# Range tests made in the second layer's stage on data loaded a second time, no clamps, and border decays multiplied on VectorE

## The chip, the cores and the metric

The kernel runs on one NeuronCore of a Trainium2 chip. The core has five engines that run side by side and wait for each other through semaphores: TensorE (PE in the profile; its weight loads are PEld), VectorE (DVE), ScalarE (ACT), GpSimd (POOL) and SyncE (SP), which here only starts DMA transfers. The metric is the device time of one launch in microseconds (us), as a median of three runs.

## The reference

Three blocks follow each other. The first is a linear attention with a complex decay: 4 batches, 8 heads, 768 steps, head size 48. The two others are feed-forward layers on the 3072 x 384 result.

```
mag = sqrt(a_re^2 + a_im^2);  scale = min(mag, 0.999) / (mag + 1e-6)
S   = (a * scale)_t * S + k_t v_t^T          # complex state per head, 48 x 48
y_t = q_t . Re(S)
g   = elu(y @ w_in);    x2  = g @ w_out                         # d_ff 2048
h   = max(x2 @ w1, x2 @ w2, x2 @ w3);  out = h @ w_out2         # d_ff 768
```

## The kernel before

**Attention.** Time is cut into chunks of 128 steps; a pair of chunks of one batch is a group `n` (12 groups), and its chunks are `(n, 0)` and `(n, 1)`. In each group the decay is turned into a logarithm and an angle (`sq`, `m2`, `lns`, `inv0` to `inv2`, `rho`, `wexp`, `lnr`, `arctan`), both are summed along time with a matmul (`cum_t`, `cum_l`), and `q` and `k` are multiplied by exp(+-) of the sums and by cosine and sine (`emul`, `hat`). Then come the transposes, masked scores, the state and the output `y`, which `x_split` writes as two fp32r halves into the tile `x` of the first layer. Between neighbouring chunks the state is scaled by a border decay: `rate` writes half of it, `gain` multiplies it twice with a row of exp tiles (tile `gt`, 32 x 384), sends one row to DRAM (`gd`) and reads it back as the tile `g` (48 x 8, two transfers), which `state_out` needs.

**First layer.** Columns of 256 tokens (block `b`, 12 of them, one per group) go through 16 weight tiles `w0` to `w15`. A step `(b, j)` uses two of them: `h_pair` (line 705) makes the hidden values, `elu` and `elu_split` turn them into `g`, `o_pair` (line 748) adds into `x2`. Weights arrive as 64-bit words; `dec1` puts each together on VectorE (`word`, lines 190 to 197), copies it on ScalarE (line 83) and subtracts the copy (line 204).

**Range tests.** The fast path holds only while the decays lie in a range and the weights have exponents in a range. `chk_re` and `chk_im` are ScalarE operations with an accumulated sum into `flags`; the test of a weight is a VectorE operation on its top bytes (line 212, tile `dm`) and a ScalarE sum into `small`. `clamp` (line 266) and `clamp_im` (line 273) on VectorE hold `re` and `im` inside the range for the work that follows. At the end all marks are added, and a general version of the program runs if one is set.

**Second layer.** `m_step(b, f)` (line 957) makes three banks of 128 x 512 with 27 matmuls, `ScalarE` copies the first (tile `t`), VectorE takes the maximum with the second and the third (lines 965, 966), and the result is split into the tile `m`. Even and odd `f` use different sets of three PSUM banks. `out_step(b)` (line 981) is 72 matmuls in four groups, each copied out by ScalarE (tile `o`) from one of two banks. There are 6 blocks of 512 tokens and 6 tiles `f`; six larger weight tiles (`wb`, 1536 KB each) are decoded at the end of the first layer and at the start of the second.

**Order.** The first group is written out by hand. The others follow the table `STEPS`: each row names a relative step and functions of it, and `work_until` calls them between the steps of the first layer. What comes out is put in order by a scheduler, engine by engine, and each engine then works through its own list in that order. All transfers are started by SP, in order too: a transfer whose target buffer is still in use holds back the ones listed after it.

Of the kernel before, what the change touches and what calls it, by code (L numbers as in the profile page):

```python
# [9 lines left out]
F32 = mybir.dt.float32  # L10
F32R = mybir.dt.float32r
U32 = mybir.dt.uint32
U8 = mybir.dt.uint8
I32 = mybir.dt.int32
AF = mybir.ActivationFunctionType
ALU = mybir.AluOpType
# [4 lines left out]
P = 128  # L21
W = H * D
# [3 lines left out]
NF1, NF2, NK = FF1 // P, FF2 // P, DM // P  # L26
NT = B * S
RE_LO, IM_HI = 0.8, 0.75
# [5 lines left out]
NWA, NWB = 2 * DM, 3 * NK * P + DM  # L34
# [58 lines left out]
def tile_kernel(  # L93
# [14 lines left out]
    nc = tc.nc  # L108
    act = ActQueue(tc)
# [3 lines left out]
    wp = pa.enter_context(tc.tile_pool(name="wp", bufs=1))  # L113
    mp = pa.enter_context(tc.tile_pool(name="mp", bufs=2))
# [3 lines left out]
    T = {}  # L118
# [3 lines left out]
    def at(shape, tag, dt=F32, bufs=1, name=None):  # L122
        return ap.tile(shape, dt, tag=tag, name=name or tag, bufs=bufs)
# [39 lines left out]
    def const_col(x, name):  # L163
        t = cp.tile([P, 1], F32, name=name)
        nc.vector.memset(t, x)
        return t

    b_w = const_col(math.log(2e-6), "b_w")
    b_re = const_col(RE_LO, "b_re")
    b_im = const_col(-IM_HI * IM_HI, "b_im")  # L170
    b_pi2 = const_col(math.pi / 2, "b_pi2")
    flags = cp.tile([P, 2 * NG], F32, name="flags")
# [13 lines left out]
    def word(raw, t):  # L186

        hw, lw = raw[:, :, 1], raw[:, :, 0]
        u = t.bitcast(U32)
        nc.vector.tensor_scalar(  # L190
            out=u, in0=hw, scalar1=0x07FFFFFF, scalar2=3,
            op0=ALU.bitwise_and, op1=ALU.logical_shift_left,
        )
        nc.vector.scalar_tensor_tensor(
            out=u, in0=hw, scalar=0xC0000000, in1=u, op0=ALU.bitwise_and, op1=ALU.bitwise_or
        )
        nc.vector.scalar_tensor_tensor(  # L197
            out=u, in0=lw, scalar=29, in1=u, op0=ALU.logical_shift_right, op1=ALU.bitwise_or
        )

    def split_w(wpool, t, n, tag):
        wt = wpool.tile([P, 2, n], F32R, tag=tag, name="w")
        act.copy(wt[:, 0, :], t)
        nc.vector.tensor_tensor(  # L204
            out=wt[:, 1, :], in0=t, in1=wt[:, 0, :].bitcast(F32), op=ALU.subtract
        )
        return wt

    def decode(wpool, raw, n, tag, t, m, col):

        top = raw.rearrange("p n t -> p (n t)").bitcast(U8).rearrange("p (n t) -> p n t", t=8)
        nc.vector.tensor_scalar(
            out=m, in0=top[:, :, 7], scalar1=0x78, scalar2=0x38,
            op0=ALU.bitwise_and, op1=ALU.bitwise_xor,
        )
        act.activation(m, m, AF.Identity, accum_out=small[:, col:col + 1])
        word(raw, t)
        return split_w(wpool, t, n, tag)

# [34 lines left out]
    def new(nm, n):  # L254
        if (nm, n) not in T:
            T[nm, n] = at([P, 2, W], nm)
        return T[nm, n]

    def of(nm, n, c):
        t = new(nm, n)  # L260
        return t if c is None else t[:, c, :]

    def clamp(n, c=None, to=None):
        if ("rec", n) not in T:
            T["rec", n] = T["re", n] if to is None else to
        nc.vector.tensor_scalar(
            out=of("rec", n, c), in0=of("re", n, c), scalar1=RE_LO, scalar2=2.0**30,
            op0=ALU.max, op1=ALU.min,
        )

    def clamp_im(n, c=None):
        x = of("im", n, c)
        nc.vector.tensor_scalar(
            out=x, in0=x, scalar1=-IM_HI, scalar2=IM_HI, op0=ALU.max, op1=ALU.min
        )

    def sq(n, c=None):
        act.activation(of("m2", n, c), of("rec", n, c), AF.Square)
        act.activation(of("aux", n, c), of("im", n, c), AF.Square)

    def m2(n, c=None):
        x = of("m2", n, c)
        nc.vector.tensor_tensor(out=x, in0=of("aux", n, c), in1=x, op=ALU.add)

    def chk_im(n, to=None):
        act.activation(
            new("aux", n) if to is None else to, T["aux", n], AF.Relu, bias=b_im,
            accum_out=flags[:, 2 * n + 1:2 * n + 2],
        )

    def chk_re(n, to=None):
        act.activation(
            new("aux", n) if to is None else to, T["re", n], AF.Relu, bias=b_re, scale=-1.0,
            accum_out=flags[:, 2 * n:2 * n + 1],
        )

    def lns(n, c=None):
        act.activation(of("aux", n, c), of("rec", n, c), AF.Ln)
# [111 lines left out]
    def gain(n, c):  # L410
        if ends(n, c):
            return
        n2, c2 = after(n, c)
        sl = bslice(c)
        t = T["gt", n2]
        nc.gpsimd.tensor_tensor(out=t[sl], in0=t[sl], in1=T["em", n2, c2][sl], op=ALU.mult)  # L416
        nc.gpsimd.tensor_tensor(out=t[sl], in0=t[sl], in1=T["ep", n, c][sl], op=ALU.mult)
        row = P - 1 if c == 0 else 0
        ci = 2 * n + c
        nc.sync.dma_start(gd[ci], t[row:row + 1, :])  # L420
        g = at([96, H], "g", bufs=2)
        for j in (0, 1):
            T["dma"] = nc.sync.dma_start(
                g[j * D:(j + 1) * D, :], gd[ci].rearrange("o (h d) -> d (o h)", h=H)
            )
        T["g", ci] = g
# [225 lines left out]
    def state_out_in(n):  # L652
# [2 lines left out]
    STEPS = {  # L655
        -31: ([(load_re,)], []),
        -29: ([(load_im,)], []),
        -28: ([(chk_re,)], [(clamp,)]),
        -27: ([(sq,)], [(m2,)]),
        -26: ([(chk_im,)], [(clamp_im,)]),  # L660
        -25: ([], [(win_ln,)]),
        -24: ([(inv0,), (inv1,)], [(inv2,)]),
        -22: ([(wexp,), (rho,)], []),
# [29 lines left out]
    w1 = {}  # L693
    raw = {}
# [73 lines left out]
    def dec1(f):  # L768
        if f % 2:
            t = at([P, NWB], "tb")[:, :NWA]  # L770
        else:
            t = mp.tile([P, NWA], F32, tag="dt", name="dt", bufs=1)
        m = mp.tile([P, NWA], U8, tag="dm", name="dm", bufs=1)
        w1[f] = decode(wp, raw[f], NWA, f"w{f}", t, m, f)

    raw2, pools, wbt = {}, {}, []

# [3 lines left out]

    def split_wb(f):
        t, m = (bp.tile([P, NWB], d, tag=x, name=x) for x, d in (("dt", F32), ("dm", U8)))
        wbt.append(decode(pools[f], raw2[f], NWB, f"wb{f}", t, m, NF1 + f))

    def load_x2(b, pool):
        t = bp.tile([P, 4, NK * P], F32, tag="xr", name="xr", bufs=1)
        nc.sync.dma_start(t, x2d[4 * b:4 * b + 4].rearrange("c p n -> p c n"))
        x = pool.tile([P, 2, NK, 4, P], F32R, tag="xx", name="xx", bufs=1 if pool is bp else 2)
        tv = t.rearrange("p c (m t) -> p m c t", m=NK)  # L790
        T["xx", b] = x
        for m in range(NK):
            act.copy(x[:, 0, m], tv[:, m])
            nc.vector.tensor_tensor(
                out=x[:, 1, m], in0=tv[:, m], in1=x[:, 0, m].bitcast(F32), op=ALU.subtract
            )
# [50 lines left out]
            score(0, c, hf)  # L847
            mask(0, c, hf)

    keep_re = at([P, 2, W], "nr")  # L850
    junk = at([P, 2, W], "lnr")
    for c in (0, 1):
        clamp(0, c, keep_re)
        sq(0, c)
        m2(0, c)
    chk_im(0, junk)
    with act.window():
        both(lns)
    for f in (inv0, inv1, inv2, clamp_im, rho):
        both(f)  # L860
    both(wexp)
    chk_re(0, junk)
    load_re(1)
    load_im(1)
    load_more(0, RAW1)
# [73 lines left out]
    bq = pm.enter_context(tc.tile_pool(name="bq", bufs=1))  # L939
# [34 lines left out]
    def out_step(b):  # L974
        for i in range(4):
            bank = ps.tile([P, 512], F32, tag="a", name="ob", bufs=2)
            ts = slice(i * P, (i + 1) * P)
            for f in range(NF2):
                mt = T["m", b, f]
                for s, (wt, mi) in enumerate(((0, 0), (1, 0), (0, 1))):  # L980
                    nc.tensor.matmul(  # L981
                        bank[:, :DM], lhsT=mt[:, mi, ts], rhs=wbt[f][:, wt, NWB - DM:],
                        start=f == 0 and s == 0, stop=f == NF2 - 1 and s == 2,
                    )
            o = bq.tile([P, DM], F32, tag="o", name="o", bufs=3)
            act.copy(o, bank[:, :DM])
            nc.sync.dma_start(out[(4 * b + i) * P:(4 * b + i + 1) * P, :], o)

    NB2 = NT // 512
    half = range(NF2 // 2)  # L990
    for b in (0, 1):
        for f in half:
            m_step(b, f)
            if b == 0:
                split_wb(3 + f)
    for b in range(NB2):
        for f in range(NF2 // 2 if b < 2 else 0, NF2):
            m_step(b, f)
            if b and f == (NF2 // 2 if b == 1 else 1):
                out_step(b - 1)  # L1000
            if f == NF2 // 2 and 2 <= b + 1 < NB2:
                load_x2(b + 1, bq)
    out_step(NB2 - 1)

    count = NG * 2
# [3 lines left out]
        out=sums, in0=sums, scalar=0.0, in1=ones[:, :count], op0=ALU.mult, op1=ALU.add  # L1009
# [3 lines left out]
        out=flags, in0=flags, scalar=0.0, in1=sums, op0=ALU.not_equal, op1=ALU.add  # L1013
# [300 lines left out]
```

## Time and profile before

| | |
|---|---|
| median of 3 runs | 948.45 us (947.55 to 948.99) |
| the profiled execution | 947.95 us, of which 946.2 us are the span from the first to the last instruction |
| TensorE busy | 897.1 us (95%), weight loads 818.5 us (87%) |
| VectorE, ScalarE, GpSimd busy | 611.7 us (65%), 527.6 us (56%), 58.2 us (6%) |
| mean granted TensorE clock | 0.986 of full speed |
| DMA | 77.39 MB, mean 82 GB/s |

A busy share is a mean over stages with different limits, so the stages are read one by one: up to about 141 us the first groups of attention and the decoding of the weights go on while TensorE gets its first work; up to 640 us attention and the first layer run together; from 640 us on it is the second layer alone. Matmuls are pipelined, and a busy TensorE is not TensorE at its peak. The granted clock has two levels, 1.2 and 2.4 GHz; 1.00 in a row is 2.4 GHz throughout.

### The profile page before, as it was taken

How to read it: one execution, taken by the hardware profiler on the slowest of the kernel's cores; microseconds unless marked ns; L12 is line 12 of the kernel's file. 1: busy time of each engine (PE TensorE's matmuls, PEld its weight loads, DVE VectorE, ACT ScalarE, POOL GpSimd, SP SyncE). 2: the span in 40 equal slices, each digit the busy share in tenths (PEclk: the TensorE clock that was granted, in tenths of full speed). 3: DMA queues.
4: the chain of work that ended last, by engine and by line, in shares of the span. 5: the costliest groups of instructions: out<-in, count | busy, mean ns of one | idle time of the engine just before them, and what ended most of it. 6: DMA issues, size and time to landing. Idle time of an engine off the chain costs nothing.

```text
span 946.2 us, 19146 instructions
## 1 busy us (share of the span) xinstructions
PE 897.1 (95%) x8036; PEld 818.5 (87%) x8036; DVE 611.7 (65%) x938; ACT 527.6 (56%) x857; POOL 58.2 (6%) x45
## 2 busy tenths in 40 slices
PE   4568989999999999999999999999999999999997
PEld 1448879999999999999999999998888989898886
DVE  6997999988877897878786753687822141322221
ACT  8988888876766786766763633665312121221111
POOL 0110120011100120200020200000000000000000
PEclk9987989999999999999999999999999999999999
DMA  8642011253333333333323212616101102000001
GB/s 320 263 182 79 1 46 46 72 139 90 100 81 96 80 96 79 97 80 96 79 63 80 63 46 52 250 35 250 34 9 42 50 1 66 2 26 9 17 17 38
DMA packets 63943, 77.39 MB, mean 82 GB/s; under 512 B 22100, under 2 KB 51944, under 8 KB 63080
## 3 DMA queue, kind: packets, MB, share of 16 engines
q1 hardware_dynamic: 63848, 76.08, 26.4%
q8 instruction: 65, 1.06, 0.5%
q14 instruction: 30, 0.25, 0.1%
HBM read 52.43 MB, written 9.47 MB: 65 GB/s over the span
## 4 chain that ended last, share of the span: by engine, by line
PE 84%; DVE 7%; ACT 6%; DMA 1%; issue 1%; POOL 1%; SPq 0%; DVEq 0%; ACTq 0%; POOLq 0%
PE mb L957 24%; PE x L748 20%; PE h L705 19%; PE ob L981 8%; PE a L585 4%; PE a L530 4%; PE a L553 3%; PE a L352 1%; ACT L78 1%; ACT aux L78 1%; DVE w L204 1%; DVE lnr L328 1%; PE a L527 1%; DVE dt L197 1%; ACT dm L78 1%
## 5 line engine op out<-in xcount | busy, mean ns | idle before, releaser
L705 PE MATMUL h<-x,w 128*128 128x256 f32 x1728 | 233.5, 287 | 5.7 <-ACT w L83 3.0
L748 PE MATMUL x<-g,w 128*128 128x256 f32 x1728 | 233.9, 287 | 0.1
L705 PEld LDWEIGHTS h<-x,w 128*128 128x128 f32 x1728 | 218.5, 193 | 11.7 <-ACT w L83 3.6
L748 PEld LDWEIGHTS x<-g,w 128*128 128x128 f32 x1728 | 217.4, 192 | 9.0 <-issue 6.5
L957 PE MATMUL mb<-xx,w 128*128 128x512 f32 x972 | 224.8, 392 | 0.0
L957 PEld LDWEIGHTS mb<-xx,w 128*128 128x128 f32 x972 | 182.4, 188 | 40.8
L78 ACT ACTIVATE e<-h 128x512 f32<-128x512 f32 x96 | 56.9, 593 | 85.8 <-PE h L705 85.1
L965 DVE TENSOR_TENSOR t<-mb,t 128x512 f32<-128x512 f32 x36 | 24.9, 690 | 122.0 <-PE mb L957 122.0
L716 DVE SCALAR_TENSOR_TENSOR e<-e,h 128x512 f32<-128x512 f32 x96 | 65.1, 678 | 43.7 <-ACT e L78 43.5
L83 ACT CAST m<-t 128x512 fp32r<-128x512 f32 x36 | 22.4, 621 | 119.7 <-DVE t L966 119.7
L83 ACT CAST g<-e 128x512 fp32r<-128x512 f32 x96 | 59.2, 616 | 47.3 <-DVE e L716 47.1
L725 DVE TENSOR_TENSOR g<-e,g 128x512 fp32r<-128x512 f32 x96 | 65.8, 685 | 19.5 <-ACT g L83 19.2
L981 PE MATMUL ob<-w,m 128*128 128x384 f32 x432 | 76.4, 337 | 0.0
L981 PEld LDWEIGHTS ob<-w,m 128*128 128x128 f32 x432 | 75.6, 188 | 0.5
L78 ACT ACT_TABLE_LOAD x54 | 69.3, 1283 | 1.7 <-PEq L1298 0.7
L78 ACT ACTIVATE e<-e 128x512 f32<-128x512 f32 x96 | 60.7, 632 | 2.2
L416 POOL TENSOR_TENSOR gt<-gt,em 32x384 f32<-32x384 f32 x20 | 31.0, 1548 | 473.1 <-ACT em L78 428.1
L966 DVE TENSOR_TENSOR t<-mb,t 128x512 f32<-128x512 f32 x36 | 24.9, 691 | 39.4 <-PE mb L957 39.4
L83 ACT COPY o<-ob 128x384 f32<-128x384 f32 x24 | 11.5, 479 | 59.3 <-PE ob L981 59.3
L530 PE MATMUL a<-qkt 96*32 96x128 f32 x1152 | 38.9, 276 | 0.7 <-DVE p L539 0.7
L83 ACT COPY t<-mb 128x512 f32<-128x512 f32 x36 | 21.1, 586 | 33.1 <-PE mb L957 24.6
L969 DVE TENSOR_TENSOR m<-t,m 128x512 fp32r<-128x512 f32 x36 | 24.9, 691 | 20.3 <-ACT m L83 20.3
(114 smaller groups left out, 1052.1 us busy)
## 6 DMA issues: line engine op xcount, KB each, us to landing
qkt<-tb SPq DMA_DIRECT2D x216, 64.0 KB
raw<-in_wa_dram SPq DMA_DIRECT2D x16, 768.0 KB
raw<-in_wb_dram SPq DMA_DIRECT2D x6, 1536.0 KB
v<-in_v_dram SPq DMA_DIRECT2D x24, 256.0 KB
q<-in_q_dram SPq DMA_DIRECT2D x12, 384.0 KB
k<-in_k_dram SPq DMA_DIRECT2D x12, 384.0 KB
x2d<-x SPq DMA_DIRECT2D x36, 128.0 KB
xr<-x2d SPq DMA_DIRECT2D x6, 768.0 KB
```

Source lines behind the costliest of these rows:

```text
L78: ins = self.nc.scalar.activation(out, in_, func, **k)
L83: self.nc.scalar.copy(out, in_)
L416: nc.gpsimd.tensor_tensor(out=t[sl], in0=t[sl], in1=T["em", n2, c2][sl], op=ALU.mult)
L530: nc.tensor.matmul(o[32 * s:32 * s + 32], lhsT=k1[:, s], rhs=q1, start=True, stop=True, tile_position=(0, 32 * s),)
L553: nc.tensor.matmul(bank[:96, h * D:(h + 1) * D], lhsT=kh[:, h, :], rhs=vt[:, o:o + D], start=True, stop=True,)
L585: nc.tensor.matmul(bank[32 * quad:32 * quad + 32, o * P:(o + 1) * P], lhsT=lhs, rhs=rhs, start=start, stop=stop, tile_position=(0, 32 * quad),
L705: nc.tensor.matmul(bank[:, i * BT:(i + 1) * BT], lhsT=w[:, wi, wsl], rhs=xb[b][:, xi, kk, :], start=m == 0, stop=m == 8,)
L716: nc.vector.scalar_tensor_tensor(out=e, in0=e, scalar=-1.0, in1=bank, op0=ALU.add, op1=ALU.max)
L725: nc.vector.tensor_tensor(out=g[:, 1], in0=e, in1=g[:, 0].bitcast(F32), op=ALU.subtract)
L748: nc.tensor.matmul(x2[m], lhsT=w[:, wi, wsl], rhs=g[:, gi, i * BT:(i + 1) * BT], start=j + i + s == 0 and b > 1, stop=j == NP - 1 and i == ...
L957: nc.tensor.matmul(bank, lhsT=wbt[f][:, wt, o:o + P], rhs=x[:, xi, kk].rearrange("p c t -> p (c t)"), start=m == 0, stop=m == 8,)
L981: nc.tensor.matmul(bank[:, :DM], lhsT=mt[:, mi, ts], rhs=wbt[f][:, wt, NWB - DM:], start=f == 0 and s == 0, stop=f == NF2 - 1 and s == 2,)
```

## The change

Three things are changed. The functions `clamp`, `clamp_im`, `chk_re` and `chk_im` go; the tile `rec` is now `re` itself. The test of the first layer's weights leaves `decode` (now `fit`). In the second layer's stage, all of `a_re` and `a_im` (12 groups of twice 384 KB) and the first layer's 16 weight tiles (768 KB each) are loaded once more, and the tests are made there: per group two ScalarE operations with a sum and one square, per weight tile one VectorE and one ScalarE operation. And `gain` multiplies on VectorE. The tests of the second layer's own weights stay where they were.

```
-    def decode(wpool, raw, n, tag, t, m, col):
+    def fit(raw, m, col):
         top = raw.rearrange("p n t -> p (n t)").bitcast(U8).rearrange("p (n t) -> p n t", t=8)
         nc.vector.tensor_scalar(
             out=m, in0=top[:, :, 7], scalar1=0x78, scalar2=0x38,
             op0=ALU.bitwise_and, op1=ALU.bitwise_xor,
         )
         act.activation(m, m, AF.Identity, accum_out=small[:, col:col + 1])
+    def decode(wpool, raw, n, tag, t):
         word(raw, t)
         return split_w(wpool, t, n, tag)
...
     def sq(n, c=None):
+        T["rec", n] = T["re", n]
...
-        nc.gpsimd.tensor_tensor(out=t[sl], in0=t[sl], in1=T["em", n2, c2][sl], op=ALU.mult)
-        nc.gpsimd.tensor_tensor(out=t[sl], in0=t[sl], in1=T["ep", n, c][sl], op=ALU.mult)
+        nc.vector.tensor_tensor(out=t[sl], in0=t[sl], in1=T["em", n2, c2][sl], op=ALU.mult)
+        nc.vector.tensor_tensor(out=t[sl], in0=t[sl], in1=T["ep", n, c][sl], op=ALU.mult)
...
-        -28: ([(chk_re,)], [(clamp,)]),
         -27: ([(sq,)], [(m2,)]),
-        -26: ([(chk_im,)], [(clamp_im,)]),
...
-        w1[f] = decode(wp, raw[f], NWA, f"w{f}", t, m, f)
+        w1[f] = decode(wp, raw[f], NWA, f"w{f}", t)
...
+    again, fits = [], list(range(NF1))
+    def load_again():
+        f = len(again)
+        if f < NF1:
+            t = bq.tile([P, NWA, 2], U32, tag="again", name="again", bufs=3)
+            nc.sync.dma_start(t.rearrange("p n t -> p (n t)"), wa[:, f, :].bitcast(U32))
+            again.append(t)
+    def in_range(n):
+        for i, src in enumerate((a_re, a_im)):
+            t = bq.tile([P, 2, W], F32, tag=f"rng{i}", name="rng", bufs=2)
+            nc.sync.dma_start(t, src[n])
+            mark = flags[:, 2 * n + i:2 * n + i + 1]
+            if i == 0:
+                act.activation(t, t, AF.Relu, bias=b_re, scale=-1.0, accum_out=mark)
+            else:
+                act.activation(t, t, AF.Square)
+                act.activation(t, t, AF.Relu, bias=b_im, accum_out=mark)
+    def fit_again():
+        if fits:
+            f = fits.pop(0)
+            fit(again[f], bq.tile([P, NWA], U8, tag="fm", name="fm", bufs=2), f)
+            load_again()
...
+            if b == 1 and f >= NF2 // 2:
+                load_again()
+            if b > 1:
+                fit_again()
+                if f % 2:
+                    in_range((b - 2) * NF2 // 2 + f // 2)
```

Three places show what the scheduler makes of it. The first is ScalarE in the first stage, group 0, from the second table load on (`lnr,flags` and `aux,flags` are `chk_re`, `dm,small` is the test of a weight, `th` the arctan, `gt` the border rate):

```order
 L78 ACT_TABLE_LOAD
 L78 ACTIVATE aux<-aux 128x384 x2
-L78 ACTIVATE lnr,flags<-re,b_re 128x768
-L78 ACTIVATE dm,small<-dm 128x768
-L78 ACTIVATE aux<-m_125,b_w 128x384 x2
+L78 ACTIVATE aux<-m_122,b_w 128x384 x2
 L78 ACT_TABLE_LOAD
 L78 ACTIVATE th<-th 128x384 x2
 L78 ACT_TABLE_LOAD
 L78 ACTIVATE gt<-lnr 32x384 x2
-L78 ACTIVATE aux,flags<-re,b_re 128x768
```

The tests are gone from between the steps of the decay; the two operations on `m` follow the exponentials directly.

The second place is SP's list of transfers at the first border decay (`gd` and `g` are its way through DRAM, `k` and `q` the inputs of group 1, `raw` the first layer's weights):

```order
 L181 DMA raw<-in_wa_dram 128x1536 x6
-L420 DMA gd<-gt 1x384
-L423 DMA g<-gd 48x8x1 x2
+L398 DMA gd<-gt 1x384
+L251 DMA k<-in_k_dram 128x768
+L247 DMA q<-in_q_dram 128x768
+L401 DMA g<-gd 48x8x1 x2
 L181 DMA raw<-in_wa_dram 128x1536 x8
```

The loads of `k` and `q` for group 1 now stand between the write of `gd` and the reads of `g`, and ahead of eight weight tiles that they stood behind.

The third place is ScalarE of the changed kernel in the second layer, at the ends of the fourth and fifth `m_step` (`t<-mb` frees a PSUM bank, `m<-t` splits a result, `rng` are the tests on the data loaded again):

```order
L83 COPY t<-mb 128x512
L83 CAST m<-t 128x512
L78 ACTIVATE rng,flags<-rng,b_re 128x768
L78 ACTIVATE rng<-rng 128x768
L78 ACTIVATE rng,flags<-rng,b_im 128x768
L78 ACTIVATE rng,flags<-rng,b_re 128x768
L83 COPY t<-mb 128x512
L78 ACTIVATE rng<-rng 128x768
L83 CAST m<-t 128x512
L78 ACTIVATE rng,flags<-rng,b_im 128x768
L83 CAST w<-dt 128x1536
L78 ACTIVATE rng,flags<-rng,b_re 128x768
```

The first tests stand as early as the fifth `m_step`, between the copies that free banks; the last of them stands behind the first copy `o` of the second `out_step`, and all 16 weight tests lie in the same stretch.

## Rows read from the trace of the kernel before

**Rows 1.** Windows: PE, PEld, DVE, ACT, POOL busy (instructions), PEclk, DMA share, GB/s

```profile
0.00:50.50 50.50, 26.61 (x192) 16.79 (x192) 41.26 (x70) 45.12 (x73) 3.90 (x7) 1.00 0.79 300
50.50:94.60 44.10, 32.78 (x320) 28.89 (x321) 39.09 (x60) 38.99 (x62) 7.00 (x4) 0.81 0.32 109
94.60:141.00 46.40, 40.69 (x297) 38.20 (x296) 44.46 (x67) 40.33 (x68) 9.57 (x4) 0.93 0.09 24
141.00:640.00 499.00, 497.48 (x5826) 476.82 (x5825) 383.31 (x597) 331.03 (x535) 37.75 (x30) 1.00 0.32 86
640.00:702.30 62.30, 62.30 (x272) 50.70 (x271) 42.79 (x56) 23.98 (x36) 0.00 (x0) 1.00 0.29 108
702.30:752.50 50.20, 50.20 (x254) 45.57 (x253) 11.45 (x17) 10.34 (x19) 0.00 (x0) 1.00 0.13 44
```

**Rows 2.** Timeline of TensorE: start, length, instruction [idle time before it, releaser]

```profile
50.53 0.50 PE L705 MATMUL h<-x,w 128*128 128x256 f32 x2 [0.31 <-ACT x L83]
...
68.47 1.92 PE L490 MATMUL a<-cst,qh 128*96 128x128 f32 x8 [7.69 <-DVE qh L469]
...
94.64 4.48 PE L705 MATMUL h<-x,w 128*128 128x256 f32 x36
...
130.20 0.50 PE L705 MATMUL h<-x,w 128*128 128x256 f32 x2 [3.00 <-ACT w L83]
```

**Rows 3.** Windows of TensorE alone, around its slow clock

```profile
68.40:81.00 12.60, 9.54 (x49) 0.52 0.18 47
...
133.30:137.00 3.70, 3.70 (x18) 0.50 0.12 1
```

**Rows 4.** Timeline of ScalarE, first stage

```profile
29.84 0.51 ACT L78 ACTIVATE em<-a 128x384 f32<-128x384 f32 x1
```

**Rows 5.** Groups by form, whole span: busy us, mean ns | idle time before

```profile
L78 ACT ACTIVATE dm<-dm 128x768 uint8<-128x768 uint8 x16 | 13.5, 841 | 1.5 <-DVE dm L212 1.3
...
L78 ACT ACTIVATE aux<-aux,b_im 128x768 f32<-128x768 f32 x11 | 10.3, 935 | 7.3 <-DVE m L283 7.3
...
L78 ACT ACTIVATE aux<-im 128x768 f32<-128x768 f32 x11 | 9.2, 840 | 0.0
```

**Rows 6.** Timeline of GpSimd, first pair of border multiplications

```profile
30.50 1.49 POOL L416 TENSOR_TENSOR gt<-gt,em 32x384 f32<-32x384 f32 x1 [22.30 <-ACT em L78]
32.07 1.60 POOL L417 TENSOR_TENSOR gt<-gt,ep 32x384 f32<-32x384 f32 x1
```

**Rows 7.** Timeline of VectorE: one form beside GpSimd's work and away from it

```profile
31.05 1.75 DVE L469 TENSOR_TENSOR kh<-k,cs 128x768 f32<-128x768 f32 x1
...
39.27 0.95 DVE L469 TENSOR_TENSOR kh<-k,cs 128x768 f32<-128x768 f32 x1
```

**Rows 8.** Groups of VectorE from 51.5 to 94.7 us

```profile
L212 DVE TENSOR_SCALAR dm<-raw 128x768 uint8<-128x768 uint8 x4 | 3.0, 751 | 0.0
...
L389 DVE SCALAR_TENSOR_TENSOR th<-nr,cst,th 32x384 f32<-32x384 f32 x2 | 1.2, 608 | 0.0
L266 DVE TENSOR_SCALAR re<-re 128x768 f32<-128x768 f32 x2 | 1.1, 554 | 0.0
...
L311 DVE TENSOR_TENSOR re<-re,aux 128x768 f32<-128x768 f32 x1 | 1.0, 957 | 2.5 <-ACT aux L78 2.5
```

**Rows 9.** Groups of VectorE from 94.7 to 141 us

```profile
L212 DVE TENSOR_SCALAR dm<-raw 128x768 uint8<-128x768 uint8 x7 | 3.9, 553 | 0.0
L204 DVE TENSOR_TENSOR w<-dt,w 128x768 fp32r<-128x768 f32 x3 | 3.7, 1221 | 0.0
L204 DVE TENSOR_TENSOR w<-tb,w 128x768 fp32r<-128x768 f32 x3 | 3.2, 1066 | 1.4 <-ACT w L83 1.4
```

**Rows 10.** Chain that ended last, second layer: start, length, what

```profile
640.13 62.36 PE mb L957 x270
...
739.94 12.57 PE ob L981 x72
```

**Rows 11.** Windows of the queue engine SP: DMA share and GB/s

```profile
643.00:652.00 9.00, 1.00 0.93 359
```

More of the change, by code (lines that the diff above doesn't have):

```diff
@@ L261, in of @@
         return t if c is None else t[:, c, :]
[L263 to L275, printed above, removed]
     def sq(n, c=None):
+        T["rec", n] = T["re", n]
         act.activation(of("m2", n, c), of("rec", n, c), AF.Square)
@@ L283, in m2 @@
         nc.vector.tensor_tensor(out=x, in0=of("aux", n, c), in1=x, op=ALU.add)
[L285 to L295, printed above, removed]
     def lns(n, c=None):
@@ L772, in dec1 @@
             t = mp.tile([P, NWA], F32, tag="dt", name="dt", bufs=1)
-        m = mp.tile([P, NWA], U8, tag="dm", name="dm", bufs=1)
-        w1[f] = decode(wp, raw[f], NWA, f"w{f}", t, m, f)
+        w1[f] = decode(wp, raw[f], NWA, f"w{f}", t)
     raw2, pools, wbt = {}, {}, []
@@ L783, in split_wb @@
         t, m = (bp.tile([P, NWB], d, tag=x, name=x) for x, d in (("dt", F32), ("dm", U8)))
-        wbt.append(decode(pools[f], raw2[f], NWB, f"wb{f}", t, m, NF1 + f))
+        fit(raw2[f], m, NF1 + f)
+        wbt.append(decode(pools[f], raw2[f], NWB, f"wb{f}", t))
     def load_x2(b, pool):
@@ L848, in scores0 @@
             mask(0, c, hf)
-    keep_re = at([P, 2, W], "nr")
-    junk = at([P, 2, W], "lnr")
     for c in (0, 1):
-        clamp(0, c, keep_re)
         sq(0, c)
         m2(0, c)
-    chk_im(0, junk)
     with act.window():
         both(lns)
-    for f in (inv0, inv1, inv2, clamp_im, rho):
+    for f in (inv0, inv1, inv2, rho):
         both(f)
     both(wexp)
-    chk_re(0, junk)
     load_re(1)
```

## The prediction

> **What bounds the kernel now.** I read the time by stage first, since the shares of the whole span hide it [rows 1]. From 141 to 640 us TensorE is busy for 497.48 of 499.00 us, and from 640 to 752 us without a gap. There its stream of matmuls sets the end, and the change leaves that stream as it is: what is taken from VectorE or ScalarE there gains nothing, what is added costs nothing while results leave PSUM in time. Before 141 us it is otherwise. Up to 50.5 us TensorE is busy for 26.61 us, from there to 94.6 us for 32.78 of 44.10, and to 141 us for 40.69 of 46.40, part of it at half clock, while VectorE is busy for 39.09 and 44.46 us of the last two stretches and ScalarE for 45.12 of the first 50.5. So the first 141 us are paced by VectorE and ScalarE, and only that can move the end.
>
> The timeline of TensorE shows what it lacks there [rows 2]. The first layer cannot start before x of group 0 is split: its first matmuls start at 50.53 us. Then it waits 7.69 us for qh of group 1, until 68.47; block 1 starts with 36 matmuls in one run at 94.64, when x of group 1 is there; at 130.20 it has waited 3.00 us for a weight tile. After the long gap and after this one the granted clock falls: 0.52 from 68.4 to 81 us, 0.50 from 133.3 to 137, which is the 1.2 GHz level, where 18 matmuls took 3.70 us [rows 3].
>
> **Term 1, the way to the first x.** ScalarE works in one chain from 6 us to the border exponentials, the last of which starts at 29.84 us [rows 4]. In front of it go: chk_im and chk_re of group 0, chk_re of group 1 and two weight tests; the chk_im of group 1 stands right behind it. A check takes 0.94 us and a weight test 0.84 [rows 5], without the small reads of the sums: 3 x 0.94 + 2 x 0.84 = 4.5 us. Part of it is covered, as ScalarE would wait for VectorE in some of these places (the two operations on m need VectorE's inverse): I take 3.5. The border decay then goes to VectorE. GpSimd needed 1.49 + 1.60 us for the first pair [rows 6]. VectorE is the dearer engine, but the trace has its price for the same shape: the 32 x 384 operation of line 389, 1.2 us for two, 0.6 each [rows 8]. And VectorE was slower beside GpSimd: kh took 1.75 us at 31.05, and 0.95 at 39.27 without it [rows 7], 0.8 lost on one of the two operations that overlap the pair. So a pair costs VectorE 1.2 us and gives back 0.8 to 1.6: about nothing for VectorE, and 3.1 - 1.2 = 1.9 us sooner for gd. That is not kept: g is now listed behind the loads of k and q, which must wait until VectorE has read the old q and k, and on VectorE state_out waits for g with both x_splits behind it. So I count nothing for the border decay here. Term 1 is 3.5 us; its bounds are 0 (g late by all of it) and 6.4 (all of 4.5 and the 1.9).
>
> One rule of the Trainium skill bears on this. SBUF — State Buffer, section "Who interferes with whom", says that VectorE with two SBUF inputs and GpSimd reading SBUF exclude each other: the second fully blocks until the first is done. By it, the pair of rows 6 would stop VectorE for 3.1 us and not for 0.8 to 1.6, and the five pairs before 141 us would give back some 7 us more. The 1.75 us of kh beside a 1.49 us multiplication shows a delay, not a full stop, so the sum leaves this out.
>
> **Term 2, from the first x to the point where TensorE is full.** Between 51.5 and 141 us VectorE loses 4 + 7 weight tests, 3.0 + 3.9 us; five clamps (two of re and one of im in the first part, one of each in the second) at 0.55 each, 2.8 us; and what GpSimd's work cost it, of which the largest piece is line 204: three of them at 1221 ns where 0.95 is the rule, 0.8 us. It gains four pairs of border multiplications (the 4 + 4 operations of GpSimd [rows 1]), 8 x 0.6 = 4.8 us. That is 6.9 + 2.8 + 0.8 - 4.8 = 5.7 us less work [rows 8, 9]. Its waits for ScalarE were 2.5 us for the exponential of group 2 and 1.4 for a weight copy [rows 8, 9]. ScalarE loses ten weight tests and five checks there, 10 x 0.84 + 5 x 0.94 = 13 us, so I let these 3.9 us go too. Sum 9.6; I take 9, as something else is late for some of it. Lower bound 2 (the waits stay and half of the rest is taken by other late data), upper bound 15: TensorE's own waiting and slow clock in this stretch, 44.10 - 32.78 + 46.40 - 40.69 = 17 us [rows 1], less 2 that no order removes. q and k of group 1 now load ahead of eight weight tiles and don't hold anything up.
>
> **Term 3, the second layer.** Per group the tests cost ScalarE 2 x 0.94 + 0.84 = 2.7 us, 12 groups 32 us, 16 weight tests 13.5: 46 us [rows 5]. Ten m_steps took 62.36 us, one 6.24, and the second out_step began at 739.94 [rows 10]; so the tests stand between 667 (after the first bank of the fifth m_step) and 743 us (after the first quarter of that out_step) in the old time. ScalarE is busy for 23.98 + 10.34 us from 640 to 752.5 [rows 1], so there is room, and VectorE's 16 x 0.55 = 9 us have it as well. Behind a test on ScalarE stand the copies that free banks; such a copy may be late, as the first bank of a set, full after a third of its step, is written again two steps after its start, 10 us later. SP starts 40 transfers more; one that waits for its buffer holds up the x2 load of block 3, which is not needed before block 2 is done. Data: 28.3 MB are listed behind 643 us (three wb tiles, two loads of x2, 12.6 MB of weights, 9.4 of decays). Three wb tiles and an x2 load moved at 359 GB/s [rows 11]; the first test wants 8.3 MB, so at 666 us, when its turn is at 667. I count 0, bounds 0 and +3.
>
> Terms 1 to 3: 3.5 + 9 = 12.5 us. From 947.95 of the profiled execution that leaves 935.45; the median of the runs stands 0.5 us above it, so the forecast is 936.
>
> **Rivals.** (a) TensorE fills up sooner: VectorE's relief also removes the slow clock, so term 1 is 5 and term 2 is 15: 948.45 - 20 = 928.5. For it: both slow stretches follow a wait [rows 2, 3]. Against it: VectorE is then still busy for 9 tenths. (b) The relief is spent: g behind k and q takes term 1 away, and with VectorE full [rows 1] term 2 stays at 6: 948.45 - 6 = 942.5. (c) The other side: the tests wait for their data in front of bank copies, and TensorE stands in the second layer. The loads must be through by 743 + 10 = 753 us, 28.3 MB in 110 us, 257 GB/s; below 28.3 / 122.5 = 231 GB/s the wait eats the gain. At 200 GB/s they take 141.5 us, 31.5 too long, so 936 + 31.5 = 967.5. For it: the second layer's own mean was 108 GB/s [rows 1]. Against it: that stage had little to load, and where it had, it moved 359 [rows 11]. TensorE: Matmul & The Clock Gate, section "Architectural detail: the array is 16× 32×32, not 1× 128×128", says that ScalarE's queue is strictly first in, first out, which is what (c) rests on.
>
> **How the numbers follow.** Forecast 0.60, (a) 0.14, (b) 0.18, (c) 0.06, and 0.02 that it comes out even. A difference below 0.2%, 1.9 us, cannot be told from none. The forecast's own range is 932 to 940; with most of (a) and (b) it is 928 to 943.5. All but (c) and the even case are faster: 0.91 faster, 0.03 the same, 0.06 slower.
>
> **What would show it.** TensorE's first h at 46 to 48 us, block 1 at 86 to 90 in place of 94.64, the 3.00 us wait gone or below 1, the second layer's start near 628 with its 306 us unchanged, and ScalarE never idle before a bank copy for a load. I am wrong if the first h still starts at 50, if TensorE waits as long between 50 and 141 us, or if the second layer shows TensorE idle.

## The result and the profile after

The changed kernel took 938.61 us (median of 4 runs, 935.79 to 941.66) against 948.10 for the kernel before: a ratio of 0.9888, 95% interval 0.9867 to 0.9908. In a later session it took 938.9 (0.9905, 0.9884 to 0.9926). The forecast was 936, range 928 to 943.5. The profile below is of the slowest of the four runs, 941.66 us with a span of 939.7; a second profile, of a run of 936.54 us, comes with the first experiment.

The windows of the changed kernel, with the columns of [rows 1]:

```profile
0.00:50.50 50.50, 28.21 (x148) 18.61 (x152) 36.05 (x61) 38.58 (x58) 0.81 (x5) 0.94 0.77 282
50.50:94.60 44.10, 37.77 (x380) 32.73 (x373) 40.97 (x63) 34.49 (x50) 0.00 (x0) 0.84 0.37 130
94.60:141.00 46.40, 43.03 (x350) 40.98 (x350) 42.98 (x66) 35.45 (x55) 0.00 (x0) 1.00 0.09 24
141.00:640.00 499.00, 497.02 (x5795) 475.72 (x5794) 375.65 (x611) 314.40 (x500) 0.00 (x0) 1.00 0.33 89
640.00:702.30 62.30, 62.30 (x280) 51.84 (x280) 46.35 (x59) 44.19 (x79) 0.00 (x0) 1.00 0.81 303
```

ScalarE is relieved (38.58 for 45.12 in the first stretch, 35.45 for 40.33 in the third), VectorE less so (40.97 for 39.09 in the second, 42.98 for 44.46 in the third), since it has GpSimd's work now. TensorE is busier up to 141 us, and its clock no longer falls after 94.6. The clock of the first row can't be set against [rows 1]: a profile's clock records begin late (at 36.1 us before, at 34.3 here), and a window counts what lies ahead of them as 1.00. How fast TensorE ran there is told by its matmuls, under run 2. The tests show as ScalarE's 44.19 for 23.98 and as 303 GB/s for 108 after 640 us.

TensorE's timeline, the rows that answer to [rows 2], and the longest wait after 94 us:

```profile
52.92 0.50 PE L681 MATMUL h<-x,w 128*128 128x256 f32 x2 [0.61 <-ACT x L83]
...
62.32 1.05 PE L468 MATMUL a<-cst,qh 128*96 128x128 f32 x8 [1.25 <-DVE qh L447]
...
94.22 4.78 PE L681 MATMUL h<-x,w 128*128 128x256 f32 x36
...
114.64 0.91 PE L327 MATMUL a<-lnr,sums_r 128*128 128x384 f32 x2 [1.78 <-ACT em L78]
```

The first h is 2.4 us later than before, not earlier; the gap of 7.69 us before qh is down to 1.25, and the 3.00 us wait is gone. The late first h begins with a late g, as SP's and VectorE's timelines show:

```profile
30.93 0.31 SPq L398 DMA_DIRECT2D gd<-gt  x1
35.91 0.35 SPq L251 DMA_DIRECT2D k<-in_k_dram  x1
36.78 0.33 SPq L247 DMA_DIRECT2D q<-in_q_dram  x1
37.20 0.90 SPq L401 DMA_DIRECT2D g<-gd  x2
```

```profile
43.82 0.55 DVE L548 TENSOR_TENSOR s<-a,g 96x384 f32<-96x384 f32 x1 [2.79 <-DMA g<-gd]
```

gd starts at 30.93 (before: 33.69), but the reads of g are issued only at 37.20, behind the k and q that wait for VectorE, and land at 43.8. From 44.5 to 51.3 us TensorE then ran at a granted clock of 0.50, while before it had 1.00 from 43 to 52.

In the chain that ended last, the second layer starts at 633.36 in place of 640.13 and runs 306.3 us to the end of the span, 0.3 more than before (946.2 - 640.13 = 306.07):

```profile
633.36 62.36 PE mb L928 x270
695.73 12.58 PE ob L952 x72
...
739.52 6.57 PE ob L952 x36
746.09 37.29 PE mb L928 x162
```

From 695.73 to 746.09 are 50.36 us, where the kernel before took 50.01 from 702.50 to 752.51: a bank copy o stood behind the last tests.

### The profile page after: what moved, and what is told of

Read it like the earlier page. It is cut to its first block, busy times and chain, and to the rows that moved or that the text cites. A ratio compares the mean times of both kernels' runs of the same rounds, so it can differ in the third digit from the quotient of the medians.

```text
span 939.7 us, 19152 instructions
## 1 busy us (share of the span) xinstructions
PE 899.0 (96%) x8036; PEld 820.3 (87%) x8036; DVE 604.2 (64%) x952; ACT 536.8 (57%) x869; POOL 0.8 (0%) x5
## 4 chain that ended last, share of the span: by engine, by line
PE 85%; DVE 6%; ACT 4%; DMA 3%; issue 1%; SPq 0%; DVEq 0%; ACTq 0%
PE mb L928 21%; PE x L724 21%; PE h L681 20%; PE ob L952 7%; PE a L563 5%; PE a L508 4%; PE a L531 3%; DMA rng<-in_a_im_dram 2%; PE a L330 1%; PE a L505 1%; ACT rng L78 1%; PE a L468 1%; ACT L78 1%; ACT aux L78 1%; DMA g<-gd 1%
## 5 line engine op out<-in xcount | busy, mean ns | idle before, releaser
L724 PE MATMUL x<-g,w 128*128 128x256 f32 x1728 | 230.3, 286 | 1.8 <-ACT x L83 1.4
L517 DVE TENSOR_TENSOR p<-a,sums_r 128x512 f32<-128x512 f32 x48 | 32.6, 683 | 10.7 <-PE a L508 8.1
L563 PE MATMUL a<-p,v 128*32 128x128 f32 x768 | 35.1, 283 | 0.3 <-DVE p L517 0.2
```

The source lines that it names most:

```text
L517: nc.vector.tensor_tensor(out=t, in0=bank.rearrange("p (i t) -> p i t", i=4), in1=keep[c].unsqueeze(1).to_broadcast([P, 4, P]), op=ALU.mult,)
L563: nc.tensor.matmul(bank[32 * quad:32 * quad + 32, o * P:(o + 1) * P], lhsT=lhs, rhs=rhs, start=start, stop=stop, tile_position=(0, 32 * quad),
L724: nc.tensor.matmul(x2[m], lhsT=w[:, wi, wsl], rhs=g[:, gi, i * BT:(i + 1) * BT], start=j + i + s == 0 and b > 1, stop=j == NP - 1 and i == ...
```

## The experiments

Medians are set against the runs of the kernel before of the same session (948.4 to 948.7). The scheduler puts the work in order anew after each edit, and in runs 2, 3 and 5 to 10 other operations of VectorE and ScalarE moved with the edited ones before 141 us (in run 5 a weight copy `w<-dt` of ScalarE, for one, starts at 52.37 in place of 63.92 us). Only runs 1, 4 and 12 keep the changed kernel's order up to the second layer, and run 11 keeps that of run 5 but for the edited writes and, from 305 us on, a few neighbours on VectorE. So the others price an edit together with its new order.

**1. The changed kernel again.** No edit.

> The changed kernel once more, as the base for the others of this call and for a second profile. The four times so far spread over 5.9 us (935.79 to 941.66), and the profiled one is the slowest. Theory A (the spread comes from the transfers of the first stage, above all the read of g, which took 6.16 us behind k and q): the start of the second layer moves with the time (633.4 at 941.7), and where the read of g is shorter the first h starts before 52.9. Rival B (the spread comes from the second layer, whose tests wait for their data): the second layer's start stays within 1 us of 633 and its length moves away from 306. Median expected 938.6, between 936.5 and 940.5.

938.9 us, six runs from 936.54 to 942.87; the profiled one is the fastest. VectorE's state_out, TensorE's first h and the chain:

```profile
41.63 0.55 DVE L548 TENSOR_TENSOR s<-a,g 96x384 f32<-96x384 f32 x1 [1.06 <-DMA g<-gd]
```

```profile
49.12 0.50 PE L681 MATMUL h<-x,w 128*128 128x256 f32 x2 [0.63 <-ACT x L83]
```

```profile
628.40 62.36 PE mb L928 x270
```

g was there 2.2 us sooner, the first h 3.8 us, the second layer 5.0 us. Two more profiles have the same order up to the second layer (runs 4 and 12 below): state_out at 44.14 and 41.91, first h at 52.74 and 48.15, second layer at 633.52 and 629.53. From the first h to the second layer the four took 580.4, 579.3, 580.8 and 581.4 us. So the spread of the times sits ahead of the first h, with the read of g, as theory A has it. The clock goes with it: the first h differs by 3.6 to 4.8 us where g differs by some 2, and from 43 to 52 us the granted clock was 0.62 in the two late profiles, 0.81 and 1.00 in the two early ones.

**2. g ahead of q and k.**

```
+    def behind_g(ins, n):
+        if n == 1:
+            in_order(tc, ins, T["dma"])
+            T["dma"] = ins
...
+        behind_g(nc.sync.dma_start(T["q", n], q[n]), n)
...
             gain(0, 0)
-            load_more(0, NF1)
...
+    load_q(1)
+    load_k(1)
+    load_more(0, NF1)
```

> The changed kernel with the loads of q and k of group 1 listed behind the reads of g, all else in its order for the first 40 operations of every engine. Theory A (g behind k and q holds the first x back, and an earlier first x carries through): g lands at 35 to 36 in place of 43.8 us, the first h starts at 47.5 to 49.5 in place of 52.9, and the time falls by 2.5 to 4.5 us: 934 to 936. Rival B (VectorE's and ScalarE's total of work until 141 us sets the end, and the early start is spent by waits for weight tiles): the first h is earlier all the same, but the time stays within 1.5 us of the changed kernel's, 937 to 940.

939.23 us (0.9896, 0.988 to 0.9912), five runs from 938.18 to 940.15: narrower, not faster. state_out waited for nothing at 41.53, but the first h came at 49.88, for TensorE ran at half clock in the first group up to 41.3 us (windows; the clock is the third last number):

```profile
24.00:41.00 17.00, 12.60 (x72) 11.17 (x76) 14.43 (x20) 12.50 (x19) 0.00 (x0) 0.51 0.50 185
```

The changed kernel left the half clock at 34.3 us and the kernel before at 36.1, where their first records stand. Ahead of that their matmuls ran at half clock too, though windows show 1.00: these eight matmuls of the kernel before took 1.94 us, as eight like them took 1.92 at a clock of 0.52 [rows 2, 3], and 1.05 at full clock (62.32 in the timeline above).

```profile
32.86 1.94 PE L490 MATMUL a<-cst,kh 128*96 128x128 f32 x8 [8.19 <-DVE kh L469]
```

ScalarE's copies of the transposes in run 2 waited 3.40 and 1.03 us for TensorE. Neither theory foresaw this; B's time came true.

**3. The border decays alone.** Before, with `nc.gpsimd` replaced by `nc.vector` in the two lines of `gain`.

> The kernel before with one part of the change: the border decays multiplied on VectorE; clamps, checks and weight tests stay where they were. Theory A (the prediction's: eight operations more on VectorE before 141 us, some 4.6 us, against what GpSimd's accesses cost it): between 946.5 and 950. Rival B (VectorE and GpSimd exclude each other, so the multiplications on GpSimd cost VectorE their whole length, 20 us before 141 us): 940 to 944, most of the change's gain.

954.6 us, all six within 0.6 (1.0062, 1.0047 to 1.0076): slower than both theories. The first h came at 52.26, the second layer at

```profile
646.67 62.36 PE mb L957 x270
```

The way between grew by 4.8 us, from 589.6 to 594.4, about the price of the eight operations, 8 x 0.55 = 4.4. The other 1.7 us are ahead of the first h, where the clock was 0.85 from 36.1 to 50.5 us (before: 1.00); whether that is their cause was not tested.

**4. No tests in the second layer.** `load_again`, `fit_again` and `in_range` not called.

> The changed kernel without the tests of the second layer: the second loads of the decays and of the first layer's weights, and the range tests on them, are left out (their marks are set to zero), so part of the computation is missing. Theory A (the tests lie beside TensorE's work but for the 0.35 us seen in the profile): 0 to 0.6 us faster than the changed kernel. Rival B (the tests' loads and ScalarE's waits hold banks, more in other runs than in the profiled one): 1.5 to 4 us faster, and a smaller spread.

936.98 us (0.9877, 0.9858 to 0.9896). The second layer starts at 633.52 and lasts 306.0 us in the profile (span 939.5). The median is 1.9 below the changed kernel's, which lies in B's range, but the spread is no smaller (935.35 to 941.30) and the intervals overlap: the traces give the tests 0.2 to 0.3 us, the times don't exclude more.

**5. The border decays back on GpSimd**, no other edit to the changed kernel.

> The changed kernel with one part undone: the border decays are multiplied on GpSimd again. Theory A (until 141 us VectorE's work sets the pace, so the multiplications cost it their full 8 x 0.6 us, as they seem to have done alone, where the way from the first h to the second layer grew from 589.6 to 594.4 us): 932 to 935.5, that is 3.5 to 6.5 us faster than the changed kernel. Rival B (with clamps and weight tests gone VectorE has room, and GpSimd's later gd delays g): 937.5 to 941. For both: g is still listed behind q and k.

950.81 us (1.0018, 1.0005 to 1.0032), 12 us slower than the changed kernel; both theories fell. GpSimd, VectorE, ScalarE and TensorE, a timeline of each:

```profile
123.97 7.04 POOL L395 TENSOR_TENSOR gt<-gt,ep 32x384 f32<-32x384 f32 x1
```

```profile
130.07 0.68 DVE L692 SCALAR_TENSOR_TENSOR e<-e,h 128x512 f32<-128x512 f32 x1
134.61 0.69 DVE L701 TENSOR_TENSOR g<-e,g 128x512 fp32r<-128x512 f32 x1 [3.86 <-ACT g L83]
```

```profile
132.28 1.05 ACT L78 ACTIVATE gt<-lnr 32x384 f32<-32x384 f32 x2 [3.92 <-DMA gd<-gt]
```

```profile
133.99 1.09 PE L468 MATMUL a<-cst,kh 128*96 128x128 f32 x4 [3.53 <-ACT qkt L83]
```

The multiplication, 0.99 to 2.23 us in the other 39 places, ended at 131.01, just after VectorE's unbroken run ended at 130.75. gd waits for it, ScalarE's next gt (one buffer) for gd, the copies qkt and g behind that in ScalarE's queue, VectorE and TensorE for them.

It is the waiting that was new, and not the slow multiplication. The kernel before had one of 5.35 us, and ScalarE's next gt, 17 us after its end, waited for nothing (GpSimd's and ScalarE's timelines of the kernel before):

```profile
114.17 5.35 POOL L416 TENSOR_TENSOR gt<-gt,em 32x384 f32<-32x384 f32 x1 [40.78 <-ACT em L78]
```

```profile
136.57 1.04 ACT L78 ACTIVATE gt<-lnr 32x384 f32<-32x384 f32 x2
```

The Trainium skill, SBUF — State Buffer, section "Who interferes with whom", has VectorE and GpSimd exclude each other and the second blocked until the first is done. These rows agree for GpSimd as the second, but here it was held over ten operations of VectorE in a row and not over one. The reverse, which the prediction weighed (VectorE stopped by GpSimd), did not pay when it was taken away: run 3 gained nothing by it.

The second layer starts at 639.85 and lasts 309.6 us: here the tests cost 3.5 us of the 12. ScalarE waited for their data, and behind it a copy o and TensorE:

```profile
714.04 0.84 ACT L78 ACTIVATE fm<-fm 128x768 uint8<-128x768 uint8 x1 [5.03 <-DVE fm L212]
...
740.39 0.94 ACT L78 ACTIVATE rng<-rng,b_re 128x768 f32<-128x768 f32 x1 [1.33 <-DMA rng<-in_a_re_dram]
```

```profile
747.71 8.12 PE L952 MATMUL ob<-w,m 128*128 128x384 f32 x36 [1.77 <-ACT o L83]
```

The three kernels with all tests and GpSimd's border decays have such waits (309.6 us here, 307.1 in run 8, 307.9 in run 11), the others don't (306.0 to 306.3), with SP's list in that stage the same. Why is not shown.

**6. The weight tests alone.** Before, with `fit` taken out of `decode`, and `load_again` and `fit_again` in the second layer.

> The kernel before with one part of the change: the tests of the first layer's weights go to the second layer on weights loaded again; clamps and checks stay, the border decays stay on GpSimd. Theory A (VectorE loses 11 x 0.55 to 0.75 us and ScalarE 10 x 0.84 us between the first h and 141 us, all of it on the path): 939 to 943. Rival B (the weight tests stood beside waits for other data): 944.5 to 948. Neither expects a cost in the second layer above 0.5 us.

944.73 us (0.9961, 0.9943 to 0.998), 3.7 faster, at the edge between the two theories, just inside B. From the first h (52.03) to the second layer (637.90) it took 585.9 us, 3.7 less than before; the second layer 306.0. The first h itself came 1.5 us later than before.

**7. Checks and clamps alone.** Changed, with the weight tests back in `dec1`, no `load_again` and `fit_again`, the border decays on GpSimd.

> The kernel before with one part of the change: clamps and checks of the decays go (the tests are made in the second layer); the weight tests stay in the decoding, the border decays on GpSimd. g is listed behind q and k here too. Theory A (five clamps less are 2.8 us of VectorE, the checks 4.7 us of ScalarE, and the first x is not earlier since g waits): 943 to 946.5. Rival B (ScalarE's checks are the main thing, since they stand in front of the first x and of the exponentials): 938 to 942.

951.13 us (1.002, 1.0004 to 1.0037): slower by 2.7, which neither theory had. The profiled run is the slowest of ten (954.38; the fastest took 946.68). Its windows show TensorE at the half clock more than [rows 1] from 50.5 us on, and from 36.1 to 50.5 the clock was 0.76 (before: 1.00):

```profile
0.00:50.50 50.50, 30.11 (x191) 20.31 (x192) 36.38 (x60) 40.87 (x64) 3.20 (x7) 0.83 0.76 279
50.50:94.60 44.10, 34.64 (x265) 30.04 (x264) 40.25 (x59) 35.29 (x54) 5.09 (x4) 0.77 0.37 133
94.60:141.00 46.40, 40.64 (x321) 38.02 (x320) 42.17 (x61) 37.57 (x61) 5.55 (x4) 0.90 0.09 24
```

VectorE is busy for less than before in the first and the third (36.38 for 41.26, 42.17 for 44.46), for more in the second (40.25 for 39.09), and ScalarE for less in all three, but from the first h (51.72) to the second layer (646.53) it took 594.8 us, 5.2 more than before. Whether the clock is the cause or goes with other waits this run does not tell. The three parts alone add up to +6.1 - 3.7 + 2.7 = +5.1 us; together they gave -9.6. They don't add, and each came with an order of its own.

**8. Border decays on GpSimd and g first** (edits 2 and 5 together).

> The changed kernel with the border decays on GpSimd and the loads of q and k behind the reads of g. Theory A (both costs are real and add): 930 to 934, and the first h at 48 to 50. Rival B (an earlier g only makes TensorE idle in other places, and its clock falls, as where g alone was put first: no gain): within 1.5 us of the kernel with the border decays on GpSimd alone, whatever that is.

950.64 us (1.0015, 0.9996 to 1.0033), that is run 5 over again: B. The first h came at 52.31. GpSimd was held up twice, and ScalarE waited at the next ep, which overwrites what GpSimd reads:

```profile
62.54 7.23 POOL L403 TENSOR_TENSOR gt<-gt,em 32x384 f32<-32x384 f32 x1 [4.68 <-ACT em L78]
...
119.51 5.87 POOL L403 TENSOR_TENSOR gt<-gt,em 32x384 f32<-32x384 f32 x1 [48.07 <-ACT em L78]
```

```profile
127.10 0.49 ACT L78 ACTIVATE ep<-a 128x384 f32<-128x384 f32 x1 [2.22 <-POOL gt L404]
```

**9 and 10. TensorE's gaps filled**, in the changed kernel and with g first.

```
+    def fill(rhs, times):
+        bank = T["x2t"][0]
+        for _ in range(times):
+            nc.tensor.matmul(bank[:, :W], lhsT=none[:rhs.shape[0]], rhs=rhs, start=False, stop=False)
...
+    fill(T["nr", 0][:, 1, :], 3)
```

> The changed kernel with twelve matmuls more (zeros times a tile of 128 x 384, added to the bank of x2, which changes nothing) put into TensorE's gaps before 62 us: three behind the second nr, three behind the first ep, three behind the transposes of the second chunk, three behind the multiplied k of group 1. Theory A (much of what is left to lose before 160 us is TensorE at the half clock after its gaps, 9.4 us in the slowest profile and 4.8 in the fastest, and it delays the chain through transposes and scores): busy time at 0.5 falls below 2 us, and the time by 4 to 8 us: 930.5 to 935. Rival B (VectorE's chain sets the pace, TensorE at half clock only fills its own gaps): the clock stays up, and the time stays at 937 to 940.

> The same twelve matmuls in the changed kernel with the reads of g ahead of q and k. Theory A (the earlier g did not help because the clock fell at 24 us and the transposes of the first group ran at half clock): the first h at 47 to 48.5 in place of 49.9, the time 2.5 to 4.5 us below that of the filled kernel with g behind, 927 to 931. Rival B (the start doesn't carry through): within 1.5 us of it.

937.8 us (0.9875, 0.9849 to 0.9901) and 939.34 us (0.9898, 0.9872 to 0.9924): no gain. Rival B's time came true for run 9, though the clock did not stay up as it said; run 10 is 1.54 us above run 9, just outside its own B. The fill did its work only in the first group: windows of run 10, to be set against run 2's 0.51, and what came later:

```profile
24.00:41.00 17.00, 14.53 (x112) 10.68 (x111) 15.53 (x23) 15.18 (x24) 0.00 (x0) 1.00 0.61 207
60.00:81.00 21.00, 14.78 (x130) 12.89 (x131) 18.17 (x27) 16.08 (x23) 0.00 (x0) 0.67 0.26 66
```

The first h came at 46.27 for 49.88, block 1 at 90.00 for 92.85, the second layer at 629.51 for 632.38, in one profile each, of run 10's fastest run and run 2's slowest; the medians are equal. As the clock was not held from 60 to 81 us, the runs don't settle what it is worth there.

**11. Border decays on GpSimd, the next rate later.** Run 5, and

```
-        -17: ([(cum_t, 0), (rate,)], [(nr, 0)]),
+        -17: ([(cum_t, 0)], [(nr, 0)]),
...
-        -13: ([(cum_lx, 0), (gain_in,), (load_v, 0)], ...
+        -13: ([(cum_lx, 0), (rate,), (gain_in,), (load_v, 0)], ...
```

> The changed kernel with the border decays on GpSimd, as in the run where that cost 12 us, and one more edit: ScalarE's write of the next border rate gt stands after the exponentials ep and em of its group and not before; nothing else moves on VectorE, GpSimd or SP. Theory A (the 7.04 us that a GpSimd multiplication took beside a full VectorE hurt because ScalarE waited 3.92 us at gt, with qkt and g copies behind it): the wait at gt is gone and the time falls by 3 to 5 us, to 946 to 948. Rival B (ScalarE waits at the next ep instead, which overwrites what GpSimd reads): 949.5 to 952.

944.19 us (0.9951, 0.9936 to 0.9967): 6.6 us less than run 5, more than theory A asked. GpSimd is as slow as there, but ScalarE no longer waits at gt, and TensorE's clock stays up from 94.6 us on (GpSimd's timeline, the windows, the chain):

```profile
123.25 7.05 POOL L395 TENSOR_TENSOR gt<-gt,ep 32x384 f32<-32x384 f32 x1
```

```profile
94.60:141.00 46.40, 43.83 (x355) 41.78 (x354) 42.55 (x62) 37.85 (x57) 11.68 (x4) 1.00 0.09 24
```

```profile
633.79 62.36 PE mb L928 x270
```

With that the second layer starts where the slower profile of the changed kernel has it. Block 1 starts at 93.30 us in run 5 and 92.59 here; from there to the second layer it took 546.6 us in run 5, 541.2 here, 539.1 in all four profiles of the changed kernel's order and 545.5 before. So the wait at gt was worth 5.3 of the 7.4 us that run 5 lost on that way. Of the 5.3 us left to the changed kernel, 1.6 are in the second layer, 941.7 - 633.79 = 307.9 us against 306.3.

**12. The tests spread.**

```
+            if f > 2:
+                in_order(tc, ins, T["out", (f - 3) // 6])
...
-            nc.sync.dma_start(t, src[n])
+            in_order(tc, nc.sync.dma_start(t, src[n]), T["out", n // 3])
```

> The changed kernel with the second layer's tests spread: the second loads of block b's share stand on SP behind the output transfers of two blocks before, so that the tests fall between the fourth m_step of block 2 and the end, and no longer in one stretch up to the second out_step; nothing moves before 640 us. Theory A (TensorE lost only 0.24 and 0.35 us in the second layer in the two profiles of the changed kernel): the second layer takes 306.0 to 306.2 us, the median is 0 to 0.6 us below the changed kernel's 938.6 to 938.9. Rival B (in some runs the tests' loads come later than in those two profiles, as where GpSimd multiplied, where the second layer lost 3.6 us): 1.5 to 3 us below, like the kernel with no tests at all (936.98).

`T["out", b]` is the last output transfer of block b. 937.48 us (0.989, 0.9868 to 0.9913). The second layer takes 935.5 - 629.53 = 306.0 us, TensorE loses nothing there, as A has it; the median is 1.1 to 1.4 us below the changed kernel's, between the two theories. No version beats the changed kernel by more than its interval.

## Why the prediction was right, step by step

- **The bound.** Right. TensorE is full from 141 us on ([rows 1], and 497.02 of 499.00 after), and the whole gain lies before it.
- **Term 1, 3.5 us.** This step was mis-sized: in the four profiles with this order the first h came at 52.92, 49.12, 52.74 and 48.15, mean 50.73, 0.2 us later than [rows 2]: the term was 0. "The first h still starts at 50" was one of the prediction's own signs of being wrong, and it came true. Block 1 (89.25 to 94.37) and the second layer (628.40 to 633.52) met its other signs in the best profile alone. ScalarE's shorter chain did bring gd forward, by 2.8 us. But g behind k and q was charged only against GpSimd's 1.9 us. It is not all: with g first (run 2) the first h came only 0.6 us earlier than before, as TensorE ran at half clock up to 41.3 us. With g first and the gaps filled (run 10) it came 4.3 us earlier, in one profile, and the second layer no earlier than in the best profile of the changed kernel (629.51 and 628.40).
- **The price of GpSimd to VectorE.** The prediction read the 1.75 us of kh as "a delay, not a full stop", against 1.49 us of the multiplication. But when kh began at 31.05, only 0.94 us of that multiplication were left, and kh lost 0.80; the next operation lost 0.8 to the second multiplication in the same way. So both were stopped for nearly all of the overlap, which is nearer to the full stop that the prediction set aside:

```profile
32.73 1.35 DVE L462 TENSOR_TENSOR k<-k,em 128x384 f32<-128x384 f32 x1
```

- **Term 2, 9 us.** The size held: from the first h to the second layer 589.6 us before, 580.5 in the mean of four profiles, 9.1 less. From 50.5 to 141 us TensorE stood idle for 17.0 us before and for 8.4 to 11.1 in the four. The working did not hold, so that the hit is in good part luck. That VectorE "gains four pairs of border multiplications" for 4.8 us is right for an operation (0.549 us measured, x40) and for the kernel before (run 3: 4.8 us on this way). In the changed kernel, undoing the same edit costs 12 us (run 5) in place of giving some back. 6.6 of these came back when only ScalarE's write of gt was moved (run 11), and the profiles of the two put 5.3 us between block 1 and the second layer and 1.7 in the second layer. So ScalarE's wait for a stuck GpSimd is shown for some 5 of the 12; some 3 more lie in the second layer's tests, and the rest, the scheduler's other order among it, was not followed. The weight tests alone gave 3.7 us; the checks and clamps alone gave nothing and cost 2.7. How much of the 9 us each part gives in the changed kernel is not shown.
- **Term 3, 0.** Right: 0.2 to 0.3 us in the traces. Rival (c) is a real mechanism: it cost 3.5 us in run 5, and 0 in run 12.
- **Rivals (a) and (b).** The clock did not recover as (a) wanted: 0.81 to 0.92 from 50.5 to 94.6 us in the four profiles, 0.81 before. (b) had the half of it that came true, g behind q and k; its other half did not: term 2 was not spent.

So the time was met with one term too large by 3.5 us, and one whose sum was right although its parts, tried alone, came out otherwise. What stays open: which part of the change gives how much of the gain, why checks and clamps alone made the kernel slower, and what the half clock between 60 and 81 us costs.

## What to carry to other kernels

When parts of a change are priced one by one, ask for each which engine will wait for it once the others are made: a small operation on GpSimd was held up for 5.35 us in the kernel before, where ScalarE's next write came later and waited for nothing, and for 7.04 us in run 5, where ScalarE stood for 3.92 us at a single-buffered tile that it had to rewrite. Read the waits of the strictly ordered queues (here ScalarE at gt, SP at q and k) before the busy shares. Test parts both alone and undone: here the same two lines cost 6 us when added to the kernel before and saved 12 in the changed one. And where a scheduler sets the order, compare the engines' lists before a difference is put down to the edited lines alone: only the pair of runs 5 and 11 was so close that one moved write can be priced.

## What was not expected of the hardware

- A 32 x 384 multiplication on GpSimd, 1.0 to 1.6 us in most places, took up to 7.2 us while VectorE ran without pause, and 5.35 us in the kernel before already; VectorE lost some 0.8 us to it on an operation ([rows 7]).
- The reads of g, 1.5 KB each, landed 6.6 us after their issue when it came right behind two loads of 384 KB (37.20 to 43.8 in the slowest profile; about 5 in the fastest), while before they had landed in time for a state_out at 41.61 that waited for nothing; in four profiles the spans (934.7 to 939.7 us) followed their arrival.
- The matmuls ahead of 36.1 us in the kernel before, and of 34.3 in the changed one, ran at 1.2 GHz, whatever the clock of a window says there. In run 2 the clock rose to 2.4 GHz at 17.4 us already, fell again at 24.2, within 8.44 us without a matmul, and stayed at 0.50 until 41.3.
